# Exponentials of two scales in one operation, and the channels of a chunk taken in fours

## The chip, the cores and the metric

The kernel runs on one core of one Trainium2 chip. The time is device time in microseconds (us), the median of several executions. The engines are TensorE (PE; its weight loads are PEld in the profile), VectorE (DVE), ScalarE (ACT), GpSimd (POOL) and SyncE (SP), which issues transfers. Each engine has its own queue of instructions and works through it in order.

## The reference, cut to what matters

Two independent halves are computed and laid side by side in the output. Half A is attention over 8 positions with a dilation of 2, between two projections. Half B, which the change touches, is a long convolution whose kernel is made from 192 complex exponentials per channel:

```python
# A: x (2048, 640), 32 heads of 20;  idx = pos - 2*[0..7], masked where negative
logits = einsum("bhsd,bhswd->bhsw", q, k[idx]) * scale
a = (einsum("bhsw,bhswd->bhsd", softmax(logits), v[idx])) @ wo
# B: u (2048, 640); A_re, A_im, B_*, C_* (640, 192); log_dt, Dskip (640)
dt = exp(log_dt)
P = exp(dt * (A_re + 1j * A_im) * l)            # l = 0 .. 2047
K = einsum("dn,dnl,dn->dl", C, P, dt * B).real  # (640, 2048)
y = irfft(rfft(pad(u)) * rfft(pad(K)))[:2048]   # causal convolution per channel
b = y + u * Dskip
out = concatenate([a, b], -1)
```

## The kernel before

**Tiling.** The 640 channels of half B are worked in five chunks (`NCH = 5`) of 128. Channels lie in four groups g of 160; a chunk c takes 32 channels of each group, counted by u (4) and t (8), and a parameter tile holds channel (g, t) of quarter u on partition 32u + 8g + t. Before the change channel number = 160g + 40u + 5t + c, so that one partition's five chunks lie side by side in memory.

**Prologue** (`partB_prep` and its `fill`, lines 86 to 199). The parameters are loaded; log_dt gives dt (dtb, dtc), a diagonal DG = identity times dt, and TensorE's product of DG with `B_A_re` transposes and scales it into `alpha` (L149 to L155). `B_A_im` becomes phases, cut in three bf16 pieces (`hi`, `mid`, `lo`) that transfers move into the tile `LP` (L170). The products of B and C become coefficients `cn` (L189 to L193), transposed into `cT`. `fill(0, 1, ...)` does chunk 0 and `fill(1, NCH, ...)` the other four; both are traced before the chunk loop, and their instructions interleave.

**Tables of a chunk.** A power of the exponential is factored into tables, so that the 2048 powers need not be evaluated one by one: `exps_chunk` (L213) writes the real part R, one ScalarE exponential of 128x192 for each of 45 scales, and `trig_half` (L226) writes sines TA and TX of half a chunk from phases that TensorE computes (ps_ph). R and the sines need different tables of ScalarE's functions, so a table load stands before each.

**Kernel generation.** `small_half` (L265) multiplies tables into P, Q, F, G and X on VectorE, for half a chunk at a time. For each of the two quarters of a half, `y_form` (L299) makes three Y's, and `kgen_unit` (L309) contracts Y with X on TensorE (ps_k), and ScalarE copies the result to Ksb. The tag "Y" has four buffers, shared with Q; P has one buffer under the tag "P".

**Transforms.** `fwd` (L327) takes u or K through two steps of matmuls (ps_f), each followed by four ScalarE copies, A and Sg. `products` (L348) multiplies the spectra on VectorE, `inverse_a` (L364) goes half-way back into Z, stored to memory. `times_d` (L382) writes u times Dskip (UD) on VectorE, in ten pieces over chunks 0 to 3. After the loop the attention half runs on the same engines, with the last step of the inverse transform (`Inverse.part`, L642) in between; that step's matmuls (ps_ib) add UD.

**The order of the work.** The framework plans each engine's order ahead of time from dependences and estimated durations; `keep_in_program_order` holds an instruction at its place in the program, and `issue_after` holds a block's instructions behind a given one on the same engine. In the loop (L719 to L762) the exponentials of chunk c+1 are issued after the sines of the second half of chunk c, and the sines of chunk c+1's first half after those exponentials. In chunk 0 the matmuls of `unit(0, 1, 0)` are held behind those of the transform of u (L756). A tile takes over a buffer only when the readers of the tile before it have finished.

Of the kernel before, what the change touches and what calls it, by code (L numbers as in the profile page):

```python
# [10 lines left out]
A = mybir.AluOpType  # L11
# [5 lines left out]
NCH = 5  # L17
# [34 lines left out]
    return F1, F64  # L52


R_MULT = [float(a) for a in range(8)] + [8.0 * b for b in range(8)] + [64.0 * (16 + i) for i in range(16)] + [64.0 * (31 - i) for i in range(16, 32)]
L1_OF_ROW = [16 + i for i in range(16)] + [31 - i for i in range(16, 32)]


# [27 lines left out]
def partB_prep(tc, pools, prm):  # L86
# [9 lines left out]
    alpha = flat[:, 9824:11744].bitcast(f32).rearrange("p (c u w) -> p c u w", c=NCH, u=4)  # L96
    V.memset(flat[96:128, 0:7680].bitcast(f32), 1.0019378662109375)
    ldt = pa.tile([128, NCH], bf16, name="ldt")
    lsrc = prm["B_log_dt"].rearrange("(g u t c) -> u g t c", g=4, u=4, t=8)
    late = tc.keep_in_program_order  # L100
    one = pa.tile([128, 2], f32, name="one")
    nc.gpsimd.memset(one[:], 0.0)
# [2 lines left out]
    nat = {}  # L105
    F1n, F64n = table_consts_np()

    def load(nm):
        nat[nm] = (pa if nm == "B_A_im" else pb).tile([128, NCH, 192], bf16, name=nm, tag=nm)
        src = prm[nm].rearrange("(g u t c) n -> u g t (c n)", g=4, u=4, t=8)  # L110
        for u in range(4):
            queue = {"B_A_re": (nc.scalar, nc.sync)[u % 2], "B_A_im": nc.gpsimd, "B_B_im": nc.gpsimd, "B_C_im": nc.gpsimd}.get(nm, nc.sync)
            late(queue.dma_start(out=nat[nm][32 * u:32 * u + 32].rearrange("p c n -> p (c n)"), in_=src[u]))

    load("B_A_re")
    load("B_A_im")
    late(nc.sync.dma_start(out=CF1, in_=inline(nc, F1n, "c_F1")))
    late(nc.sync.dma_start(out=CF64, in_=inline(nc, F64n, "c_F64")))
    late(nc.scalar.activation(out=one[:], in_=one[:], func=ACT.Exp))
    for nm in ("B_B_re", "B_B_im", "B_C_re", "B_C_im"):  # L120
        load(nm)
# [13 lines left out]
    def fill(c0, c1, between):  # L135
# [60 lines left out]
            nc.scalar.copy(out=cT[:, c0:c1, 12 * u:12 * u + 12, 0:3:2], in_=ps.rearrange("p c w (q f) -> p c q w f", f=4))  # L196

        transposed(coefficients, cn, lambda sl, c: id32[sl, :])
    return dict(CF1=CF1, CF64=CF64, LP=LP, alpha=alpha, cT=cT), fill


def coefficients(engine, B, c):
# [7 lines left out]
        engine.tensor_copy(out=co[:, :, 3], in_=co[:, :, 0])  # L210


def exps_chunk(tc, pools, B, c):  # L213
    nc = tc.nc
    R = pools["tab"].tile([128, 48, NE_R, 4], bf16, name="R", tag=f"R{c % 2}")
    src = B["alpha"][:, c].rearrange("p u (q f) -> p (u q) f", f=4)
    nc.gpsimd.memset(R[:, :, 0:16:8, :], 1.0)
    nc.gpsimd.memset(R[:, :, 47, :], 1.0)
    for e, m in enumerate(R_MULT):
        if m == 0.0:  # L220
            continue
        nc.scalar.activation(out=R[:, :, e, :], in_=src, func=ACT.Exp, scale=m)  # L222
    return R


# [83 lines left out]
def kgen_unit(tc, pools, u, X, Ys, Ksb):  # L309

    nc = tc.nc
    MM = nc.tensor.matmul
    ps = pools["psum"].tile([128, 8, 64], f32, name="ps_k", tag="bank", bufs=2)
    for k in range(3):
        for t in range(8):
            for g in range(4):
                q, f = divmod(8 * g + t, 4)
                MM(ps[32 * g:32 * g + 32, t], lhsT=X[:, q, 2 - k, :, f], rhs=Ys[k][:, q, :, f], start=(t == 0 and k == 0), stop=False, tile_position=(0, 32 * g), skip_group_check=True)  # L318
        for t in range(8):
            for g in range(4):  # L320
# [61 lines left out]
def times_d(tc, pools, C, UDd, c, i):  # L382

    nc = tc.nc
    U = C["U"][:].rearrange("p l (ut c) -> p c l ut", c=NCH)[:, c]
    UD = pools["tabb"].tile([128, 32, 32], bf16, name="UD", tag="UD")
    tc.keep_in_program_order(nc.vector.tensor_tensor(out=UD[:], in0=U[:, 32 * i:32 * i + 32], in1=bc(C["Dsb"][:, c], 1, 32), op=A.mult))
    nc.sync.dma_start(out=UDd[c, :, 1024 * i:1024 * i + 1024], in_=UD[:].rearrange("p l j -> p (l j)"))


def fwd_u(tc, pools, C, Sd, c):

    U = C["U"][:].rearrange("p l (ut c) -> p c l ut", c=NCH)[:, c]
    Su, last = fwd(tc, pools, C, (lambda ut: U[:, :, ut]), 0, pools["fft"])
    tc.nc.sync.dma_start(out=Sd[c], in_=Su[:].rearrange("p a b c -> p (a b c)"))
    return last

# [221 lines left out]
class Inverse:  # L619
# [12 lines left out]
    def load(self, qr, c0=0, c1=NCH):  # L632
        nc = self.nc
        pool, tag = ((self.a2, "Z"), (self.att.ta, "LPC"), (self.att.a1, "prod"), (self.att.ta, "U"))[qr]
        if c0 == 0:
            self.t[qr] = pool.tile([96, 4, NCH, 16, 32], bf16, name="Z", tag=tag)
        for c in range(c0, c1):
            for ri in range(3):
                src = self.UDd[c, :, 512 * qr:512 * qr + 512] if ri == 2 else self.Zd[c, :, 2048 * ri + 512 * qr:2048 * ri + 512 * qr + 512]
                (nc.sync, nc.gpsimd)[(c + ri) % 2 if qr in (0, 3) else 0].dma_start(out=self.t[qr][32 * ri:32 * ri + 32, :, c].rearrange("p g l n -> p g (l n)"), in_=src.rearrange("(g p) n -> p g n" if ri == 2 else "(p g) n -> p g n", g=4))  # L640

    def part(self, l0, n):  # L642
        nc = self.nc
        qr, l = divmod(l0, 16)
        lo = l0 % 8
        if lo == 0:
            self.ysb = self.ysbs[:, l0 // 8 % 4]
        ysb = self.ysb
        ps = self.att.one("ps_ib")
        for i in range(n):  # L650
            for g in range(4):
                self.att.MM(ps[32 * g:32 * g + 32, 160 * i:160 * i + 160], lhsT=self.HB[:, l0 + i, :], rhs=self.t[qr][:, g, :, l + i, :], start=(i == 0), stop=True, skip_group_check=True, tile_position=(0, 32 * g))
        nc.scalar.copy(out=ysb[:, lo:lo + n].rearrange("p l (ut c) -> p l ut c", c=NCH), in_=ps[:, 0:160 * n].rearrange("p (l c ut) -> p l ut c", l=n, c=NCH))
# [8 lines left out]
def body(tc, ctx, pools, prm, B_u, B_Dskip, Sd, Zd, UDd, A_x, A_wqkv, A_wo, out_a, out_b):  # L662
# [14 lines left out]
    with tc.tile_pool(name="prep_b", bufs=1) as pb, tc.tile_pool(name="prep_c", bufs=1) as pc, tc.tile_pool(name="prep_a", bufs=1) as pa, tc.tile_pool(name="psum_p", bufs=2, space=bass.MemoryType.PSUM) as psp:  # L677
        pools.update(prep_a=pa, prep_b=pb, prep_c=pc)
        B, fill = partB_prep(tc, dict(pools, psum=psp), prm)
        fill(0, 1, lambda u: None)  # L680
        Dn = pa.tile([128, 160], bf16, name="Dn")
        dsrc = B_Dskip.rearrange("(g ch) -> g ch", g=4)
        late = tc.keep_in_program_order
        late(nc.sync.dma_start(out=BD[:].rearrange("p a b n -> p (a b n)"), in_=inline(nc, cn["BD"], "c_BD")))
        late(nc.sync.dma_start(out=EA[:].rearrange("p a n -> p (a n)"), in_=inline(nc, cn["EA"], "c_EA")))
        late(nc.sync.dma_start(out=T2[:].rearrange("p a n -> p (a n)"), in_=inline(nc, cn["T2"], "c_T2")))
        for g in range(4):
            late(nc.sync.dma_start(out=Dn[32 * g:32 * g + 32, :], in_=dsrc[g].partition_broadcast(32)))
# [5 lines left out]
        nc.gpsimd.tensor_copy(out=Dsb[:], in_=Dn[:].rearrange("p (ut c) -> p c ut", c=NCH))  # L694
# [24 lines left out]
    for c in range(NCH):  # L719
# [88 lines left out]
    def fill(some, n=1):  # L808
        for f in some[0:n]:
            f()  # L810
        del some[0:n]
# [97 lines left out]
```

## Time and profile before

| What | us |
|---|---|
| median of 3 runs (439.4 to 442.8) | 439.51 |
| the profiled execution | 438.98 |
| its span, first to last instruction | 437.2 |
| VectorE busy | 391.3 (89%) |
| TensorE busy | 358.4 (82%) |
| ScalarE busy | 314.0 (72%) |
| GpSimd busy | 44.5 (10%) |

A row of the groups gives the line, engine, operation, the tiles written and read with their shapes, how often it ran, the busy time and the mean length of one, and what ended the idle time before it. A row of the timeline gives start, length, engine, line, operation and count. Queues of transfers appear as SPq or as DMA rows. A tile's name appears without its buffer's number, and tiles that share a buffer may appear under the first one's name: `alpha` and the tables of constants are shown as LPC.

### The profile page before, as it was taken

The numbers are of one execution on the slowest core, as the hardware profiler recorded it, in microseconds if no ns is written. First come the engines' busy times: TensorE is split into PE (matmuls) and PEld (weight loads), VectorE is DVE, ScalarE is ACT, GpSimd is POOL, SyncE is SP. The second block draws the span as 40 slices with busy tenths as digits, with TensorE's granted clock in tenths as the row PEclk, the third lists the DMA queues.
The fourth block names the chain that finished last, engine by engine and source line by source line (L and its number), as shares of the span: only waits on it lengthen the run. The fifth ranks groups of instructions, "written<-read, shape, count | busy, mean of one in ns | idle before, by whom it ended". The sixth has DMA issues, their size and how long they took to land.

```text
span 437.2 us, 17687 instructions
## 1 busy us (share of the span) xinstructions
PE 358.4 (82%) x8041; PEld 241.1 (55%) x8041; DVE 391.3 (89%) x386; ACT 314.0 (72%) x570; POOL 44.5 (10%) x85
## 2 busy tenths in 40 slices
PE   1397659989886998879778799999899897399995
PEld 0145546866863677556665665545555674134443
DVE  7889999999997999999999989946978989999751
ACT  3974998889999899979997845342858344544663
POOL 7440000000000000000010000400001204102110
PEclk9996577999999898889999899999999999659999
DMA  5569102163233402324079933500210907957343
GB/s 143 186 141 200 18 3 109 39 227 94 99 123 123 97 28 98 144 103 99 27 258 241 236 75 135 178 0 3 67 32 1 265 17 201 228 141 225 96 107 114
DMA packets 45131, 51.62 MB, mean 118 GB/s; under 512 B 31376, under 2 KB 38992, under 8 KB 42368
## 3 DMA queue, kind: packets, MB, share of 16 engines
q1 hardware_dynamic: 41520, 41.41, 35.4%
q0 software_dynamic: 3392, 8.95, 7.0%
q8 instruction: 63, 1.03, 1.0%
q10 hardware_dynamic: 144, 0.12, 0.1%
q14 instruction: 12, 0.10, 0.1%
HBM read 28.03 MB, written 18.35 MB: 106 GB/s over the span
## 4 chain that ended last, share of the span: by engine, by line
PE 49%; ACT 29%; DVE 14%; issue 5%; DMA 1%; SPq 1%; DVEq 0%; ACTq 0%
ACT R L222 10%; ACT A L338 6%; PE ps_k L318 6%; PE ps_ph L247 6%; PE ps_k L323 6%; PE ps_op L420 6%; PE ps_k L470 4%; PE ps_q L488 4%; PE ps_ph L250 4%; ACT Sg L344 4%; PE ps_f L343 4%; PE ps_v L501 2%; DVE prod L521 2%; ACT Z L375 2%; PE ps_o L420 2%
## 5 line engine op out<-in xcount | busy, mean ns | idle before, releaser
L305 DVE TENSOR_TENSOR Y<-F,G 128x3072 bf16<-128x3072 bf16 x60 | 102.9, 1751 | 0.6 <-PE ps_k L323 0.6
L222 ACT ACTIVATE R<-LPC 128x192 bf16<-128x192 f32 x225 | 59.3, 358 | 0.1
L247 PE MATMUL ps_ph<-LPC 128*128 128x256 bf16 (+1 forms) x200 | 41.5, 311 | 17.3 <-DMA LPC<-lo 8.7
L318 PE MATMUL ps_k<-Y,X 128*32 128x64 bf16 x1920 | 47.2, 239 | 7.3 <-DVE Y L305 3.8
L323 PE MATMUL ps_k<-Y,X 64*32 64x64 bf16 x1920 | 43.8, 233 | 3.4 <-issue 3.3
L344 ACT CAST Sg<-ps_f 128x1024 bf16<-128x1024 f32 x40 | 37.6, 1027 | 7.3 <-PE ps_f L343 7.3
L318 PEld LDWEIGHTS <-X 128*32 128x32 bf16 x1920 | 32.1, 117 | 17.4 <-issue 9.0
L343 PE MATMUL ps_f<-A,T 128*128 128x128 bf16 x320 | 27.3, 259 | 14.9 <-ACT A L338 14.2
L338 ACT CAST A<-ps_f 128x1024 bf16<-128x1024 f32 x40 | 37.6, 1036 | 0.7 <-PE ps_f L337 0.6
L271 DVE TENSOR_TENSOR X<-R,TX 128x1536 bf16<-128x1536 bf16 x40 | 36.4, 951 | 0.0
L323 PEld LDWEIGHTS <-X 64*32 64x32 bf16 x1920 | 29.6, 113 | 12.1 <-issue 4.4
L255 ACT ACTIVATE TX<-ps_ph 128x864 bf16<-128x864 int16 (+1 forms) x40 | 31.9, 867 | 5.3 <-DVE X L271 2.5
L343 PEld LDWEIGHTS <-T 128*128 128x128 bf16 x320 | 25.6, 119 | 16.1 <-issue 14.9
L585 DVE TENSOR_TENSOR prod<-v,atp 128x2048 bf16<-128x2048 bf16 (+2 forms) x32 | 31.3, 1018 | 2.0 <-PE ps_o L420 1.8
L255 ACT ACTIVATE TA<-ps_ph 128x768 bf16<-128x768 int16 x40 | 30.6, 822 | 3.4 <-PE ps_ph L250 3.0
L250 PE MATMUL ps_ph<-LPC 128*64 128x128 bf16 (+1 forms) x400 | 29.6, 249 | 0.0
L247 PEld LDWEIGHTS <-LPC 128*128 128x128 bf16 x200 | 15.0, 102 | 25.9 <-issue 19.1
L420 PE MATMUL ps_op<-wo,o 128*128 128x320 bf16 x160 | 28.5, 315 | 0.8 <-ACT o L595 0.4
L358 DVE TENSOR_TENSOR P<-P,Sg 128x4096 bf16<-128x4096 bf16 x10 | 22.9, 2288 | 4.1 <-DMA P<-Sdram 3.2
L250 PEld LDWEIGHTS <-LPC 128*64 128x64 bf16 x400 | 15.2, 118 | 19.1 <-issue 18.9
L611 ACT CAST ob<-ps_op 128x320 bf16<-128x320 f32 x28 | 11.9, 431 | 19.0 <-PE ps_op L420 17.3
L337 PE MATMUL ps_f<-BD,U 128*64 128x128 bf16 x320 | 19.4, 285 | 6.1 <-ACT A L338 3.3
(129 smaller groups left out, 661.2 us busy)
## 6 DMA issues: line engine op xcount, KB each, us to landing
Sdram<-Sg SPq DMA_DIRECT2D x5, 1024.0 KB
P<-Sdram SPq DMA_DIRECT2D x5, 1024.0 KB
P<-Sdram SPq DMA_DIRECT2D x10, 512.0 KB
Zdram<-Z SPq DMA_DIRECT2D x5, 1024.0 KB
Z<-Zdram SPq DMA_DIRECT2D x30, 128.0 KB
U<-in_B_u_dram SPq DMA_DIRECT2D x4, 640.0 KB
UDdram<-UD SPq DMA_DIRECT2D x10, 256.0 KB
out_dram<-ysb SPq DMA_DIRECT2D x32, 80.0 KB
```

The costliest lines, as they stand in the source:

```text
L222: nc.scalar.activation(out=R[:, :, e, :], in_=src, func=ACT.Exp, scale=m)
L247: MM(o[:, :, 0:32], lhsT=L[:, 0:128], rhs=rhs, start=first, stop=last, skip_group_check=True)
L250: MM(o[64 * hh:64 * hh + 64, :, 32:48], lhsT=L[:, 128:192], rhs=rhs[:, :, 16 * hh:16 * hh + 16], start=False, stop=last, skip_group_check= ...
L255: last = nc.scalar.activation(out=dst[:, qs, e0:e0 + 2 * n, :].rearrange("p q (b e) f -> p b e q f", b=2), in_=words.rearrange("p b (e q f ...
L271: TT = lambda o, a, b, op: V.tensor_tensor(out=o, in0=a, in1=b, op=op)
L305: nc.vector.tensor_tensor(out=Y[:].rearrange("p q (b a) f -> p q b a f", a=8), in0=fa, in1=gb, op=A.mult)
L318: MM(ps[32 * g:32 * g + 32, t], lhsT=X[:, q, 2 - k, :, f], rhs=Ys[k][:, q, :, f], start=(t == 0 and k == 0), stop=False, tile_position=(0, ...
L323: MM(ps[32 * g:32 * g + 32, t], lhsT=X[hb, q, 2 - k, :, f], rhs=Ys[k][hb, q, :, f], start=False, stop=(k == 2), tile_position=(64 * (g // ...
L338: nc.scalar.copy(out=A1[:, :, 32 * b:32 * b + 32].rearrange("p k (j g) -> p k j g", g=4), in_=ps[:].rearrange("p j k g -> p k j g"))
L343: last = MM(ps[:, kk], lhsT=C["T2"][:, 8 * b + kk, :], rhs=A1[:, 8 * b + kk, :], start=(kk % 4 == 0), stop=True, skip_group_check=True)
L344: nc.scalar.copy(out=Sg[:, :, 8 * b:8 * b + 8, :], in_=ps[:].rearrange("p k (j g) -> p j k g", g=4))
L420: self.MM = lambda *a, **k: self.tc.keep_in_program_order(self.nc.tensor.matmul(*a, **k))
```

## The change

Four things are edited.

1. **Exponentials.** `R_MULT` goes. The 45 scales of a chunk are sorted into pairs (m, 2m) where both are wanted: 14 pairs and 17 single ones. A pair is one ScalarE operation of 128x384 that reads a new tile `twice`, which holds 2 x alpha and alpha, and writes two rows of R. `twice` is written by VectorE for chunk 0 and by GpSimd for chunks 1 to 4; for these it lies in the buffer of tag "P". The single ones are issued first and still read `alpha`.
2. **Channel order.** Channel number is now 160g + 20t + 4c + u. The u of four neighbours is therefore adjacent in the tile of u, of Dskip and of the output; the views of U, Dsb, Ksb, ps_ib and ysb are written accordingly, and log_dt and the parameters are read with other strides.
3. **Loads.** Each parameter's chunk 0 is one transfer over 128 partitions. Its chunks 1 to 4 follow in four transfers: those of `B_A_im` and `B_A_re` at once, those of B and C after the moves of chunk 0's pieces (`load_rest`).
4. **Queues.** `B_A_re` of chunk 0 goes to ScalarE's queue, its rest to SP's; the imaginary parts stay on GpSimd's.

```diff
-R_MULT = [float(a) for a in range(8)] + [8.0 * b for b in range(8)] + [64.0 * (16 + i) for i in range(16)] + [64.0 * (31 - i) for i in range(16, 32)]
...
-    lsrc = prm["B_log_dt"].rearrange("(g u t c) -> u g t c", g=4, u=4, t=8)
+    lsrc = prm["B_log_dt"].rearrange("(r c u) -> u r c", c=NCH, u=4)
...
+    def load(nm, queue, rest):
+        if not rest:
+            nat[nm] = (pa if nm == "B_A_im" else pb).tile([128, NCH, 192], bf16, name=nm, tag=nm)
+            late(queue.dma_start(out=nat[nm][:, 0], in_=prm[nm].rearrange("(r c u) n -> c u r n", c=NCH, u=4)[0]))
+        else:
+            src = prm[nm].rearrange("(r c u) n -> u r c n", c=NCH, u=4)
+            for u in range(4):
+                late(queue.dma_start(out=nat[nm][32 * u:32 * u + 32, 1:], in_=src[u, :, 1:]))
+    load("B_A_im", nc.gpsimd, False)
+    load("B_A_re", nc.scalar, False)
...
+    load("B_A_im", nc.gpsimd, True)
+    load("B_A_re", nc.sync, True)
+    def load_rest():
+        for nm, queue in (("B_B_re", nc.sync), ("B_C_re", nc.sync), ("B_B_im", nc.gpsimd), ("B_C_im", nc.gpsimd)):
+            load(nm, queue, True)
...
-def exps_chunk(tc, pools, B, c):
+def exps_chunk(tc, pools, B, c, engine, twice):
...
+    alpha = B["alpha"][:, c].rearrange("p u w -> p (u w)")
+    for b in range(2):
+        engine.tensor_scalar(out=twice[:, b], in0=alpha, scalar1=2.0 - b, scalar2=None, op0=A.mult)
...
-    for e, m in enumerate(R_MULT):
-        if m == 0.0:
-            continue
-        nc.scalar.activation(out=R[:, :, e, :], in_=src, func=ACT.Exp, scale=m)
+    one, two = [], []
+    for places in ({a: a for a in range(1, 8)}, {8 * a: 8 + a for a in range(1, 8)}, {64 * j: j if j > 15 else 47 - j for j in range(1, 32)}):
+        left = sorted(places)
+        while left:
+            m = left.pop(0)
+            e, step = places[m], 0
+            if 2 * m in left:
+                left.remove(2 * m)
+                step = places[2 * m] - e
+            (two if step else one).append((m, e, step))
+    for m, e, step in one + two:
+        src = twice[:].rearrange("p b (q f) -> p q b f", f=4)
+        if step == 0:
+            src, out = alpha.rearrange("p (q f) -> p q f", f=4), R[:, :, e, :]
+        elif step < 0:
+            out = R[:, :, e + step:e + 1:-step, :]
+        else:
+            src, out = src[:, :, ::-1, :], R[:, :, e:e + step + 1:step, :]
+        nc.scalar.activation(out=out, in_=src, func=ACT.Exp, scale=float(m))
...
-    nc.scalar.copy(out=Ksb[:, 8 * u:8 * u + 8, :], in_=ps[:])
+    nc.scalar.copy(out=Ksb.rearrange("p (t u) l -> p u t l", u=4)[:, u], in_=ps[:])
...
-    U = C["U"][:].rearrange("p l (ut c) -> p c l ut", c=NCH)[:, c]
+    U = C["U"][:].rearrange("p l (t c u) -> p c l t u", c=NCH, u=4)[:, c]
...
-        fill(0, 1, lambda u: None)
+        fill(0, 1, lambda u: B["load_rest"]() if u == 3 else None)
...
-        R[0] = exps_chunk(tc, pools, B, 0)
+        R[0] = exps_chunk(tc, pools, B, 0, nc.vector, pa.tile([128, 2, 192], f32, name="twice"))
...
+            twice = pools["tabb"].tile([128, 2, 192], f32, name="twice", tag="P")
             with tc.issue_after(trig[c, 1][2].ins):
                 coefficients(nc.scalar, B, c + 1)
-                R[c + 1] = exps_chunk(tc, pools, B, c + 1)
+                R[c + 1] = exps_chunk(tc, pools, B, c + 1, nc.gpsimd, twice)
```

More of the change, by code (lines that the diff above doesn't have):

```diff
@@ L106, in partB_prep @@
     F1n, F64n = table_consts_np()
[L108 to L116, printed above, removed]
+    def load(nm, queue, rest):
[8 more added lines that the diff above has]
+    load("B_A_re", nc.scalar, False)
+    late(nc.scalar.activation(out=one[:], in_=one[:], func=ACT.Exp))
     late(nc.sync.dma_start(out=CF1, in_=inline(nc, F1n, "c_F1")))
     late(nc.sync.dma_start(out=CF64, in_=inline(nc, F64n, "c_F64")))
-    late(nc.scalar.activation(out=one[:], in_=one[:], func=ACT.Exp))
-    for nm in ("B_B_re", "B_B_im", "B_C_re", "B_C_im"):
-        load(nm)
+    for nm, queue in (("B_B_re", nc.sync), ("B_B_im", nc.gpsimd), ("B_C_re", nc.sync), ("B_C_im", nc.gpsimd)):
+        load(nm, queue, False)
+    load("B_A_im", nc.gpsimd, True)
[3 more added lines that the diff above has]
+            load(nm, queue, True)
     dtb = pa.tile([128, NCH], bf16, name="dtb")
@@ L198, in fill @@
         transposed(coefficients, cn, lambda sl, c: id32[sl, :])
-    return dict(CF1=CF1, CF64=CF64, LP=LP, alpha=alpha, cT=cT), fill
+    return dict(CF1=CF1, CF64=CF64, LP=LP, alpha=alpha, cT=cT, load_rest=load_rest), fill
 def coefficients(engine, B, c):
@@ L210, in coefficients @@
         engine.tensor_copy(out=co[:, :, 3], in_=co[:, :, 0])
-def exps_chunk(tc, pools, B, c):
+def exps_chunk(tc, pools, B, c, engine, twice):
     nc = tc.nc
     R = pools["tab"].tile([128, 48, NE_R, 4], bf16, name="R", tag=f"R{c % 2}")
-    src = B["alpha"][:, c].rearrange("p u (q f) -> p (u q) f", f=4)
+    alpha = B["alpha"][:, c].rearrange("p u w -> p (u w)")
+    for b in range(2):
+        engine.tensor_scalar(out=twice[:, b], in0=alpha, scalar1=2.0 - b, scalar2=None, op0=A.mult)
     nc.gpsimd.memset(R[:, :, 0:16:8, :], 1.0)
     nc.gpsimd.memset(R[:, :, 47, :], 1.0)
-    for e, m in enumerate(R_MULT):
-        if m == 0.0:
-            continue
-        nc.scalar.activation(out=R[:, :, e, :], in_=src, func=ACT.Exp, scale=m)
+    one, two = [], []
[17 more added lines that the diff above has]
+        nc.scalar.activation(out=out, in_=src, func=ACT.Exp, scale=float(m))
     return R
@@ L384, in times_d @@
     nc = tc.nc
-    U = C["U"][:].rearrange("p l (ut c) -> p c l ut", c=NCH)[:, c]
+    U = C["U"][:].rearrange("p l (t c u) -> p c l t u", c=NCH, u=4)[:, c]
     UD = pools["tabb"].tile([128, 32, 32], bf16, name="UD", tag="UD")
-    tc.keep_in_program_order(nc.vector.tensor_tensor(out=UD[:], in0=U[:, 32 * i:32 * i + 32], in1=bc(C["Dsb"][:, c], 1, 32), op=A.mult))
+    tc.keep_in_program_order(nc.vector.tensor_tensor(out=UD[:].rearrange("p l (t u) -> p l t u", u=4), in0=U[:, 32 * i:32 * i + 32], in1=bc(C["Dsb"][:, c].rearrange("p (t u) -> p t u", u=4), 1, 32), op=A.mult))
     nc.sync.dma_start(out=UDd[c, :, 1024 * i:1024 * i + 1024], in_=UD[:].rearrange("p l j -> p (l j)"))
 def fwd_u(tc, pools, C, Sd, c):
-    U = C["U"][:].rearrange("p l (ut c) -> p c l ut", c=NCH)[:, c]
-    Su, last = fwd(tc, pools, C, (lambda ut: U[:, :, ut]), 0, pools["fft"])
+    U = C["U"][:].rearrange("p l (t c u) -> p c l t u", c=NCH, u=4)[:, c]
+    Su, last = fwd(tc, pools, C, (lambda tu: U[:, :, tu // 4, tu % 4]), 0, pools["fft"])
     tc.nc.sync.dma_start(out=Sd[c], in_=Su[:].rearrange("p a b c -> p (a b c)"))
@@ L651, in part @@
             for g in range(4):
-                self.att.MM(ps[32 * g:32 * g + 32, 160 * i:160 * i + 160], lhsT=self.HB[:, l0 + i, :], rhs=self.t[qr][:, g, :, l + i, :], start=(i == 0), stop=True, skip_group_check=True, tile_position=(0, 32 * g))
-        nc.scalar.copy(out=ysb[:, lo:lo + n].rearrange("p l (ut c) -> p l ut c", c=NCH), in_=ps[:, 0:160 * n].rearrange("p (l c ut) -> p l ut c", l=n, c=NCH))
+                self.att.MM(ps[32 * g:32 * g + 32, 160 * i:160 * i + 160].rearrange("p (t c u) -> p c t u", c=NCH, u=4), lhsT=self.HB[:, l0 + i, :], rhs=self.t[qr][:, g, :, l + i, :], start=(i == 0), stop=True, skip_group_check=True, tile_position=(0, 32 * g))
+        nc.scalar.copy(out=ysb[:, lo:lo + n].rearrange("p l ch -> p (l ch)"), in_=ps[:, 0:160 * n])
         if lo + n == 8:
@@ L693, in body @@
         fill(1, NCH, lambda g: late(nc.sync.dma_start(out=U[32 * g:32 * g + 32], in_=usrc[g])))
-        nc.gpsimd.tensor_copy(out=Dsb[:], in_=Dn[:].rearrange("p (ut c) -> p c ut", c=NCH))
+        nc.gpsimd.tensor_copy(out=Dsb[:].rearrange("p c (t u) -> p c t u", u=4), in_=Dn[:].rearrange("p (t c u) -> p c t u", c=NCH, u=4))
     psg = ctx.enter_context(tc.tile_pool(name="psum_g", bufs=2, space=bass.MemoryType.PSUM))
```

## The prediction

> **What bounds the kernel now.** I read the page's busy line, then VectorE's and ScalarE's rows in time order through the chunk loop, then GpSimd's rows, then the groups by shape.
>
> From the page, and from the table of waits:
>
> ```profile
> PE 358.4 (82%) x8041; PEld 241.1 (55%) x8041; DVE 391.3 (89%) x386; ACT 314.0 (72%) x570; POOL 44.5 (10%) x85
> ...
> DVE P L271 <- ACT TA L255: 3.0, 1, 3.0
> ```
>
> From 33.87 us (the first product P of chunk 0) to 283.5 us, the end of the last Y, VectorE starts nearly every instruction before the one ahead has ended; its gaps there sum to some 6 us, the longest the 3.0 above. VectorE sets the pace of the loop, with ScalarE just behind: P of chunk c+1 waits for tables TA that ScalarE writes after the exponentials. P starts at 33.87, 75.72, 133.35, 184.28 and 233.99 us in the five chunks.
>
> VectorE, then ScalarE, where chunk 1 is prepared (start, length, line):
>
> ```profile
> 56.52 1.75 DVE L271 TENSOR_TENSOR Q<-P,cT 128x3072 bf16<-128x3072 bf16 x1
> ...
> 71.15 1.32 DVE L387 TENSOR_TENSOR UD<-U,Dsb 128x1024 bf16<-128x1024 bf16 x1
> 72.39 3.42 DVE L305 TENSOR_TENSOR Y<-F,G 128x3072 bf16<-128x3072 bf16 x2
> 75.72 0.95 DVE L271 TENSOR_TENSOR P<-R,TA 128x1536 bf16<-128x1536 bf16 x1
> ...
> 57.25 4.16 ACT L222 ACTIVATE R<-LPC 128x192 bf16<-128x192 f32 x16
> 61.31 3.72 ACT L338 CAST A<-ps_f 128x1024 bf16<-128x1024 f32 x4
> 71.20 2.30 ACT L255 ACTIVATE TA<-ps_ph 128x768 bf16<-128x768 int16 x3
> ```
>
> Behind the 16 exponentials on ScalarE's queue stand the copies A of the transform of u; TensorE's next matmuls ps_k stand behind that transform; VectorE's fifth Y of six needs the buffer of the first Y (there are four), which those matmuls free. So exponentials that start late stop all three engines.
>
> GpSimd's rows that read SBUF, and VectorE's beside them:
>
> ```profile
> 25.44 0.95 DVE L191 TENSOR_TENSOR p<-p,p 128x768 f32<-128x768 f32 x1
> 26.42 1.18 DVE L193 TENSOR_SCALAR cn<-p,dtc 128x192 bf16<-128x192 f32 x4
> ...
> 25.15 1.80 POOL L209 TENSOR_SCALAR cT<-cT 128x192 bf16<-128x192 bf16 x1 [0.54 <-ACT cT L196]
> 26.92 0.34 POOL L210 COPY cT<-cT 128x192 bf16<-128x192 bf16 x1
> ...
> 65.48 0.42 POOL L217 MEMSET R<- 128x384 bf16 x1 [35.72 <-DVE X L271]
> ...
> 276.74 6.75 DVE L305 TENSOR_TENSOR Y<-F,G 128x3072 bf16<-128x3072 bf16 x4
> 279.80 3.98 POOL L481 COPY kT<-kT 128x280 bf16<-128x280 bf16 x1 [5.74 <-ACT kT L471]
> ```
>
> A copy of 192 elements takes 0.34 us. The copy of 280 at 279.80 took 3.98 us and ended at 283.78, 0.29 after VectorE's run of tensor_tensors ended at 283.49; two instruction ends inside the run did not let it in. The tensor_scalar at 25.15 likewise sat through the end of one tensor_tensor and ended 0.56 us after the last (26.39). The memset, which reads nothing, took 0.42 under the same load.
>
> **The change, part by part.**
>
> *Exponentials.* 45 per chunk become 17 singles and 14 pairs. Before, 45 take 11.49 us, 0.255 each in a row (0.358 alone). The softmax exponential of 2048 elements takes 1.91, so an element costs (1.91-0.358)/1856 = 0.84 ns and a pair 0.255+192x0.84 ns = 0.415. New: 17x0.255+14x0.415 = 10.1 us, 1.35 less per chunk. Bounds per pair: 0.255 (nothing for the second half) to 0.51 (no gain).
>
> *The doubled copies "twice".* A pair reads a tile of two scaled copies of alpha. In chunk 0 VectorE writes it (two tensor_scalars, 0.25 each by L177). For chunks 1 to 4 GpSimd does, reading SBUF, into the buffer of P, so after Q of the half before: in chunk 1 not before 58.3 us. Each operation alone: between 0.34 (L210) and 0.56 (the end of L209 after its release); I take 0.45, 0.9 for two. On GpSimd's queue nothing urgent is behind them; on ScalarE's everything above.
>
> I take the kT row as the rule: these reads wait until VectorE has nothing to run. Then, on the clock of before (chunk by chunk):
>
> - Chunk 1. VectorE runs on from Q to the fifth Y, which it reaches at 74.06, less 0.65 for UD (below): 73.4. It stops there, since ScalarE stands at the first pair. GpSimd finishes at 74.3, 14 pairs at 80.1, four copies A (3.72) at 83.8, where before they ended at 65.03: 18.8 later. The first Y's matmuls, done near 73.1 before, are done at 91.9; fifth Y to 93.6; TA's third copy (73.5) comes at 92.3. P starts at 93.6 instead of 75.72: **+17.9**.
> - Chunk 2. VectorE, 2.5 ahead by three UDs and the 0.57 us gap of 76.7, reaches a fifth Y (125.67) before TensorE has read the first (124.57, plus 0.9 of lag). GpSimd uses that gap, at about 123.1 to 124; ScalarE wants the pairs at about 123.5. Pairs 5.8, table load 1.28, three TA 2.4: P at 133.5: **+0.2**. Without the gap it would be about +4.
> - Chunk 3. Two pairs are queued ahead of the copies Sg, so TensorE stops in the transform, VectorE at its fifth Y (179.7 less two UDs, 178.4). GpSimd 0.9, two pairs 0.8, Sg 3.8, twelve pairs 5.0, load 1.28, TA 2.4: P at 192.6, not 184.28: **+8.3**.
> - Chunk 4, the same from 230.65 less two UDs, 229.3: P at 243.4, not 233.99: **+9.4**.
>
> *u in fours.* UD's inner run becomes 4 adjacent values instead of a stride of 5. L387 takes 1.344 us for 1024 elements; L518, 1024 adjacent ones, 0.689. I take 0.69: 0.65 less on VectorE, ten times, counted in the stops above; the other end is nothing. TensorE's weight loads of U keep their stride of 160. The strided PSUM writes of ps_ib and the now contiguous copy to ysb I cost at nothing: L250 writes runs of 16 in rows of 48 and takes 249 ns, and Ksb's contiguous copy of 512 takes 580 where ysb's of 480 takes 563.
>
> *Loads.* Chunk 0's slice of each parameter comes as one 48 KB transfer, the rest after chunk 0's moves to LP. B_A_re's last quarter, landed at 9.11, no longer holds the first exponential (9.79). But log_dt now comes in pieces of 2 bytes: 640 instead of 128. At 60 ns a packet (2476 us of engine time over 41520 packets of q1), 512 more on 16 engines are up to 1.9 us; I take 1.0 (0 to 1.9). Two identity copies and tx now precede DG on VectorE, 0.6. The first exponential starts at about 10.1. ScalarE's work to the end of TX of chunk 0: 4.3+5.8 exponentials, 0.3 waiting for twice, 1.1 cT copies, 1.28 load, 3.1 TA, 0.5 alpha copies, 3.2 TX: 29.7 (30.76 before). But the order now has TX's negation ahead of 5.7 us of coefficient work (four products and sums at 0.87, eight cn at 0.27) that filled the wait before. P of chunk 0: 29.7+0.6+5.8 = 36.1, not 33.87: **+2.2**. SP's and GpSimd's later rest loads (about 27 us for the last, by 20.6 issued plus B_C_im's 5.8) and U (needed at 56, some 10 us of slack) hide behind that. Bounds -1.5 (log_dt at no cost, negation no hindrance) to +5.
>
> **Sum:** 2.2+17.9+0.2+8.3+9.4 = 38.0 us on the profiled run of 438.98 (span 437.2): 477. That run is 0.5 below the median of 439.51; behind chunk 4 nothing changes. Within the case: prep -1.5 to +5, chunk 2 up to +4, chunks 3 and 4 by 2 us each as gaps fall, pairs and UD at their dear ends +6 each, GpSimd at 0.34 to 0.56 one us: about 464 to 486.
>
> **Rivals.**
>
> 1. *GpSimd gets in at the next instruction end.* Then twice is ready at 59.2, the pairs end at 65.0 (61.41 before, +3.6), P of chunk 1 at +2.7. After that ScalarE gains 1.35 and VectorE 1.3 to 2.6 a chunk: about -3.7 over chunks 2 to 4. With +2.2 of prep: **440**, not slower. For it: only one copy shows the long block. Against: three boundaries (25.44, 280.08, 281.75), none won. [...]
> 2. *It gets in at the negation of TX* (60.46), a tensor_scalar, where no row shows GpSimd losing. Twice at 61.4, pairs 67.2, P of chunk 1 +4.9, regained in part as above: **442**. A wait of a few us in each chunk gives 445 to 464.
> 3. *Not what it says:* a pair costs two singles and UD stays: 1.35x5 and 6.5 us back, **486** with the forecast's stops.
> 4. *Both gains reach the end and prep costs nothing:* UD 6.5 less what ScalarE cannot follow, less the late start of chunk 1: about **434**.
>
> **Chances.** Forecast 0.68; rival 3 inside its upper end; 445 to 464 0.08; rivals 1 and 2 0.18; rival 4 0.06. One per cent, 4.4 us, is about what measurement of this kernel tells from no change. Slower by over that 0.76, within it 0.16, faster 0.08. The range must reach the rivals' times: 440 to 486; the forecast's own is 464 to 486.
>
> **What the profile will show.** Right: two tensor_scalars on GpSimd in chunks 1, 3 and 4 many us long, ending when VectorE falls idle; ScalarE's wait ahead of the first pair released by GpSimd, about 15 us in chunk 1; VectorE idle at the fifth Y and before P. Wrong: those rows under 1 us, P of chunk 1 near 80. Pairs near 0.415, UD near 0.69, P of chunk 0 near 36 test the rest.

## The result, and the profile after

| | before | after |
|---|---|---|
| median of 6 runs each, us | 440.19 (438.2 to 442.8) | 482.21 (480.0 to 487.0) |
| ratio, with its 95% interval | | 1.096 (1.089 to 1.103) |
| profiled execution / its span, us | 438.98 / 437.2 | 480.73 / 479.0 |

The kernel is 9.6% slower. The forecast was 477.0 within 440 to 486, slower with a chance of 0.76. On the clock of the profiled executions it said +38.0 us; they lie 41.75 apart.

From the page of the changed kernel, its busy line and three groups:

```profile
PE 361.8 (76%) x8041; PEld 241.7 (50%) x8041; DVE 387.4 (81%) x388; ACT 308.7 (64%) x500; POOL 96.7 (20%) x96
...
L333 DVE TENSOR_TENSOR Y<-F,G 128x3072 bf16<-128x3072 bf16 x60 | 103.1, 1749 | 40.0 <-PE ps_k L351 40.0
L229 POOL TENSOR_SCALAR twice<-LPC 128x192 f32<-128x192 f32 x8 | 50.7, 6345 | 170.8 <-DVE Q L299 170.8
L250 ACT ACTIVATE R<-twice 128x384 bf16<-128x384 f32 x70 | 30.0, 523 | 41.7 <-POOL twice L229 39.8
```

VectorE and ScalarE are busy for less than before (391.3 and 314.0 us there); the share of VectorE falls from 89% to 81%. Its idle time ahead of Y was 0.6 us and is 40.0; the group of Y before was:

```profile
L305 DVE TENSOR_TENSOR Y<-F,G 128x3072 bf16<-128x3072 bf16 x60 | 102.9, 1751 | 0.6 <-PE ps_k L323 0.6
```

Eight operations of 192 elements on GpSimd are busy for 50.7 us, and ScalarE's pairs wait 39.8 for them.

From the table of waits of the changed kernel (total, times, longest):

```profile
DVE Y L333 <- PE ps_k L351: 40.0, 6, 18.3
...
ACT R L250 <- POOL twice L229: 39.8, 3, 17.9
...
PE ps_f L365 <- ACT A L366: 24.8, 6, 22.6
```

That is the circle of the prediction, each engine waiting for the next. It runs in chunks 1, 3 and 4; in chunk 2 ScalarE does not wait for GpSimd. Chunk 1, from the timeline: GpSimd, then VectorE, then ScalarE (start, length, and in brackets the idle time before):

```profile
61.06 16.29 POOL L229 TENSOR_SCALAR twice<-LPC 128x192 f32<-128x192 f32 x2 [29.10 <-DVE Q L299]
...
60.82 0.55 DVE L299 TENSOR_TENSOR G<-G 128x768 bf16<-128x768 bf16 x1
61.29 0.95 DVE L299 TENSOR_TENSOR F<-Q 128x1536 bf16<-128x1536 bf16 x1
...
74.39 1.75 DVE L333 TENSOR_TENSOR Y<-F,G 128x3072 bf16<-128x3072 bf16 x1
94.47 1.76 DVE L333 TENSOR_TENSOR Y<-F,G 128x3072 bf16<-128x3072 bf16 x1 [18.33 <-PE ps_k L351]
96.14 0.95 DVE L299 TENSOR_TENSOR P<-R,TA 128x1536 bf16<-128x1536 bf16 x1
...
58.86 0.59 ACT L352 CAST Ksb<-ps_k 128x512 bf16<-128x512 f32 x1 [2.38 <-PE ps_k L351]
77.38 5.89 ACT L250 ACTIVATE R<-twice 128x384 bf16<-128x384 f32 x14 [17.94 <-POOL twice L229]
83.18 3.71 ACT L366 CAST A<-ps_f 128x1024 bf16<-128x1024 f32 x4
```

GpSimd starts 0.16 us after Q ends and finishes at 77.35, 1.2 us after VectorE's run of instructions has ended at 76.14. The shortest of the eight takes 0.68 us, the longest 15.63: where a couple is held, its first instruction is the one that stands.

Where the 41.8 us of span arise, by the start of the first product P of each chunk:

| | chunk 0 | 1 | 2 | 3 | 4 | first attention product |
|---|---|---|---|---|---|---|
| before | 33.87 | 75.72 | 133.35 | 184.28 | 233.99 | 286.48 |
| after | 36.51 | 96.14 | 153.85 | 213.37 | 273.75 | 329.78 |
| added here | +2.6 | +17.8 | +0.1 | +8.6 | +10.7 | +3.5 |
| predicted | +2.2 | +17.9 | +0.2 | +8.3 | +9.4 | 0 |

From there to the end the changed kernel takes 1.5 us less (149.2 against 150.7).

### The profile page after: what moved, and what is told of

It reads as the page before. It is cut to its first block, busy times and chain, and to the rows that moved or that the text cites. A ratio compares the mean times of both kernels' runs of the same rounds, so it can differ in the third digit from the quotient of the medians.

```text
span 479.0 us, 17629 instructions
## 1 busy us (share of the span) xinstructions
PE 361.8 (76%) x8041; PEld 241.7 (50%) x8041; DVE 387.4 (81%) x388; ACT 308.7 (64%) x500; POOL 96.7 (20%) x96
## 5 line engine op out<-in xcount | busy, mean ns | idle before, releaser
L229 POOL TENSOR_SCALAR twice<-LPC 128x192 f32<-128x192 f32 x8 | 50.7, 6345 | 170.8 <-DVE Q L299 170.8
L250 ACT ACTIVATE R<-twice 128x384 bf16<-128x384 f32 x70 | 30.0, 523 | 41.7 <-POOL twice L229 39.8
L275 PE MATMUL ps_ph<-LPC 128*128 128x256 bf16 (+1 forms) x200 | 43.6, 325 | 10.4 <-ACT TX L283 7.3
L365 PEld LDWEIGHTS <-U 128*64 128x64 bf16 x320 | 18.7, 204 | 23.2 <-issue 22.6
L278 PEld LDWEIGHTS <-LPC 128*64 128x64 bf16 x400 | 15.6, 121 | 21.8 <-issue 21.7
```

What stands on the lines that cost most here:

```text
L229: engine.tensor_scalar(out=twice[:, b], in0=alpha, scalar1=2.0 - b, scalar2=None, op0=A.mult)
L275: MM(o[:, :, 0:32], lhsT=L[:, 0:128], rhs=rhs, start=first, stop=last, skip_group_check=True)
L278: MM(o[64 * hh:64 * hh + 64, :, 32:48], lhsT=L[:, 128:192], rhs=rhs[:, :, 16 * hh:16 * hh + 16], start=False, stop=last, skip_group_check= ...
L365: MM(ps[64 * ri:64 * ri + 64, j], lhsT=src_fn(8 * b + j), rhs=C["BD"][:, wh, ri, :], start=(j % 4 == 0), stop=True, skip_group_check=True, ...
```

## The experiments

The theory, from GpSimd's 16.26 and 16.29 us in the changed kernel: a GpSimd instruction that reads SBUF stands until VectorE has a pause, and ScalarE's pairs stand behind it. The rivals: the wait is for the buffer or the queue in which `twice` lies; or the pairs, the loads or the channel order cost the time. Ratios are to the kernel before on the same chip, with 95% intervals.

| run | median, us | ratio |
|---|---|---|
| memset_twice | 444.13 | 1.006 (1.002 to 1.010) |
| singles | 448.24 | 1.017 (1.012 to 1.022) |
| scalar_twice | 448.09 | 1.015 (1.009 to 1.021) |
| pairs_alone | 491.15 | 1.117 (1.109 to 1.126) |
| early_double | 439.76 | 1.000 (0.996 to 1.004) |
| early_alone | 466.86 | 1.061 (1.054 to 1.069) |
| order_alone | 444.97 | 1.013 (1.006 to 1.019) |
| old_loads | 442.68 | 1.004 (0.999 to 1.009) |
| gap_given | 447.80 | 1.013 (1.005 to 1.020) |
| scalar_early | 443.82 | 1.003 (0.999 to 1.008) |
| pairs_scalar | 440.38 | 0.997 (0.993 to 1.002) |
| ud_alone | 439.37 | 0.996 (0.993 to 0.999) |

### GpSimd writes without reading

```diff
-        engine.tensor_scalar(out=twice[:, b], in0=alpha, scalar1=2.0 - b, ...)
+        engine.memset(twice[:, b], 0.0)      # chunks 1 to 4
```

> The changed kernel, but in chunks 1 to 4 GpSimd fills the two halves of twice with zeros by memsets instead of scaling alpha: same engine, same buffer, same place in the queues, but nothing is read from SBUF. It leaves out the doubled alpha of chunks 1 to 4, so their pairs exponentiate zeros. Theory (GpSimd's reads of SBUF wait until VectorE has nothing to run): the two memsets take under 1 us and end near 62 us in chunk 1; no stop of VectorE at the fifth Y; first products P of chunks 1 to 4 some 1 us either side of 77, 132, 182 and 232; total 435 (432 to 440), below the kernel before, since 6.5 us of UD fall away against 2.6 of preparation. Rival A (the wait is for the buffer of P, or for GpSimd's queue): the stops stay and the time is near 482. Rival B (the pairs themselves, or the loads, cost the time): near 482 as well, with P late without a stop of GpSimd.

The timeline of this run, GpSimd and ScalarE in chunk 1:

```profile
60.51 0.46 POOL L232 MEMSET twice<- 128x192 f32 x2 [29.01 <-DVE Q L302]
...
60.99 5.90 ACT L253 ACTIVATE R<-twice 128x384 bf16<-128x384 f32 x14 [2.00 <-POOL twice L232]
```

Two operations in the same buffer, behind the same Q, on the same queue: 0.46 us instead of 16.29, and 444.1 instead of 482.2 (a ratio of 1.006 instead of 1.096). So some 38 us belong to the read, or to the operation that does it, since a memset is another operation too; `gap_given` below keeps both. The total was expected at 432 to 440; it is 4 above that, and the rest of this section follows that up too. A part of it stands in the second line: ScalarE has used up its 17 single exponentials and waits 2.00 us here, because `twice` may be written only after Q has let go of the buffer of P.

### The exponentials undone

```diff
-            if 2 * m in left:
+            if False:                        # 45 single ones, no twice
```

> The changed kernel with its exponentials undone: 45 single ones per chunk that read alpha, no twice; channel order, loads and queues as changed. Theory: no stop, the time is that of before plus some 2.6 us in the preparation, less what of the 6.5 us of UD reaches the end: 437 (434 to 441). Rival B (loads or channel order cost the time): well above 445. A difference of this run to the one with memsets is what the pairs save on ScalarE's path, at most 1.35 us a chunk.

No stop, so neither loads nor order are the 42 us. But 448.2 misses the expected 434 to 441: order, loads and queues together, with UD down to 0.68 us, do not gain; they cost some 6 to 7 us (a ratio of 1.017).

### ScalarE writes twice, in the same place

```diff
+            engine.activation(out=twice[:, b], in_=alpha, func=ACT.Copy, scale=2.0 - b)
```

> The changed kernel, but in chunks 1 to 4 ScalarE itself writes twice, two copies with a scale of 128x192, into the same buffer just ahead of the pairs. All of the change's computation is done. Theory: no engine waits for another; two copies of about 0.26 us each more on ScalarE; total 436 (433 to 440), so the change without GpSimd is level with the kernel before or a little faster. Rival A (the buffer of P is what is waited for): ScalarE waits for VectorE's Q ahead of the first copy in each chunk, some us, and the time is above 445. Rival B (pairs, loads or order cost the time): near 482.

The timeline of ScalarE in this run, chunk 1:

```profile
58.10 0.59 ACT L355 CAST Ksb<-ps_k 128x512 bf16<-128x512 f32 x1 [2.38 <-PE ps_k L354]
60.18 0.62 ACT L232 ACTIVATE twice<-LPC 128x192 f32<-128x192 f32 x2 [1.49 <-DVE Q L302]
60.83 5.90 ACT L253 ACTIVATE R<-twice 128x384 bf16<-128x384 f32 x14
```

The stops are gone (448.1); the expected 433 to 440 is missed by 8. The rival on the buffer has a small part: 1.49 us for Q, and 2.38 ahead of the Ksb copy at 58.10. Before, exponentials filled both waits.

### The pairs alone, on the kernel before

The edit: the new `exps_chunk` with its calls in the kernel before, nothing else.

> The kernel before with the new exponentials alone: pairs that read twice, written by VectorE for chunk 0 and by GpSimd for chunks 1 to 4 into the buffer of P; channel order, loads and queues as before. Theory: the stops are all there, VectorE stands at the fifth Y in the chunks in which GpSimd is held: 483 (470 to 492). Where GpSimd gets in at once, as it did in chunk 2 of the changed kernel, a chunk costs nothing, so each chunk is either about 0 to 2 us or 8 to 18. Rival B (loads or order cost the time): within 1 per cent of before, 436 to 443.

Here all four chunks stop (16.85 to 21.44 us on GpSimd), and the time is higher than with the whole change. GpSimd in chunks 1 and 2, from the timeline of this run:

```profile
59.88 16.87 POOL L220 TENSOR_SCALAR twice<-LPC 128x192 f32<-128x192 f32 x2 [27.16 <-issue]
...
131.45 21.44 POOL L220 TENSOR_SCALAR twice<-LPC 128x192 f32<-128x192 f32 x2 [54.14 <-DVE Q L290]
```

Chunk 1 to 2, by the starts of P, takes 66.2 us where it took 57.6 before and 57.7 in the changed kernel, in which GpSimd was let in at once (below).

### A pause made for GpSimd

```diff
+    # on VectorE, behind F = Q0 + Q1
+    nc.vector.tensor_copy(out=scrap[:], in_=twice[:, 1, 0:1])
```

> The changed kernel with a pause made for GpSimd: behind Q's first sum F on VectorE stands a copy of one element of twice, so VectorE must wait there for GpSimd's two tensor_scalars. GpSimd, its buffer and its read of SBUF are as in the changed kernel. Theory (GpSimd is let in only when VectorE stands still): the two take about 1 to 2.5 us in every chunk, VectorE stands 0.5 to 2 us at that copy and no more at the fifth Y than in the run with ScalarE's copies; P of chunk 1 near 81; total 449 (444 to 455), some 33 us under the changed kernel though VectorE got more to do and a wait. Rival (the reads are slow of themselves beside the other engines' traffic): twice still 16 us long, VectorE stands for it at the copy, total 480 or more.

GpSimd and VectorE in chunk 1, from the timeline of this run:

```profile
60.70 2.39 POOL L257 TENSOR_SCALAR twice<-LPC 128x192 f32<-128x192 f32 x2 [28.80 <-DVE Q L305]
...
60.94 0.94 DVE L305 TENSOR_TENSOR F<-Q 128x1536 bf16<-128x1536 bf16 x1
63.13 0.15 DVE L787 COPY scrap<-twice 128x1 f32<-128x1 f32 x1 [1.25 <-POOL twice L257]
```

VectorE is given one instruction more in a chunk and made to wait 1.25 us there (0.59 in chunk 2), and the kernel becomes 34 us faster than the changed one: 447.8. The reads take 1.85 to 2.39 us in the four chunks. This shows the cause from the other side: the same operation and the same read, let in by a pause. In chunk 2 its first read was in before the pause, as in the changed kernel (below).

### The same read, a chunk earlier

GpSimd writes only the doubled alpha of chunk c+1, over alpha of chunk c, which is dead by then.

```diff
+def double(engine, B, c):
+    engine.tensor_scalar(out=B["alpha"][:, c], in0=B["alpha"][:, c + 1], scalar1=2.0, ...)
...
+        twice = B["alpha"][:, c - 1:c + 1]
```

> The whole change, with one thing moved: for chunks 1 to 4 GpSimd writes only the doubled alpha of chunk c+1, and writes it over alpha of chunk c, which lies just ahead of it and is dead once chunk c's exponentials are done. A pair reads the two neighbours; nothing lies in the buffer of P, and GpSimd has about a chunk's time instead of none. Same engine, same read of SBUF, same computation. Theory (GpSimd is held while VectorE runs without a pause, and that costs only when ScalarE waits for it): a doubling still takes up to some 16 us where VectorE runs on, but nobody waits for it; the wait of ScalarE for Q in chunk 1, 1.5 to 3.9 us in the runs with memsets and with ScalarE's copies, goes too; P of chunk 1 at 77 to 78; total 443 (438 to 448). Rival (a GpSimd that reads slows VectorE or ScalarE whenever it runs): stops or stretched instructions elsewhere, above 455.

> The kernel before with pairs in this early form alone: doubled alpha written over the chunk before by GpSimd, channel order, loads and queues as before. Theory: no stop; chunk 0 starts 1.4 us later, as in the run with pairs alone (P at 35.32), and ScalarE has 1.35 us less work a chunk: 440 (436 to 444), within one per cent of before.

> The early form of the pairs with the channel order in fours, and the loads and queues of before. Against the early form with the change's loads it tells what the loads cost. If they cost the 2 us of the preparation: 441 (436 to 445). If 384-byte pieces over all chunks load no faster than the change's slices: the same time as that run.

GpSimd, then VectorE, in the run with the whole change (`early_double`):

```profile
63.08 41.90 POOL L260 TENSOR_SCALAR LPC<-LPC 128x192 f32<-128x192 f32 x1 [30.42 <-ACT R L254]
...
178.57 4.11 POOL L260 TENSOR_SCALAR LPC<-LPC 128x192 f32<-128x192 f32 x1 [7.80 <-ACT R L254]
...
103.75 0.68 DVE L424 TENSOR_TENSOR UD<-U,Dsb 128x1024 bf16<-128x1024 bf16 x1
104.57 2.29 DVE L395 TENSOR_TENSOR P<-P,Sg 128x4096 bf16<-128x4096 bf16 x1
...
182.04 1.10 DVE L308 TENSOR_TENSOR P<-R,TA 128x1536 bf16<-128x1536 bf16 x1
```

One instruction of 192 elements stands for 41.9 us and costs nothing, for nobody needs it yet: 439.8, level with before, 42 us under the changed kernel with the same kind of read on the same engine (one instruction a chunk instead of two). It ends 0.55 us after the UD of 103.75 has ended (104.43), and the next VectorE row starts 0.14 after that end, the first gap since 63.08: a pause that short seems to be enough.

The same code on the kernel before (`early_alone`), GpSimd and ScalarE:

```profile
62.22 40.99 POOL L251 TENSOR_SCALAR LPC<-LPC 128x192 f32<-128x192 f32 x1 [24.52 <-ACT R L245]
...
177.83 54.43 POOL L251 TENSOR_SCALAR LPC<-LPC 128x192 f32<-128x192 f32 x1 [5.04 <-ACT R L245]
...
232.30 4.24 ACT L245 ACTIVATE R<-LPC 128x384 bf16<-128x384 f32 x10 [21.88 <-POOL LPC L251]
```

440 was expected and 466.9 came: a slack of a whole chunk is not enough either. The doubling for chunk 4 stood 54.43 us, past 47 ends of VectorE instructions without a pause, and ScalarE waited 21.88 for it. In `early_double` the same doubling, released at 178.57, took 4.11 us: it ended 0.55 after the end of a UD at 182.13, beside a P that took 1.10 instead of 0.95. With the loads of before (`old_loads`, median 442.7) the profiled execution took 456.07; in it that doubling was held and ScalarE waited 17.60 for it:

```profile
179.83 49.75 POOL L250 TENSOR_SCALAR LPC<-LPC 128x192 f32<-128x192 f32 x1 [7.17 <-ACT R L244]
...
229.61 2.17 ACT L244 ACTIVATE R<-LPC 128x384 bf16<-128x384 f32 x5 [17.60 <-POOL LPC L250]
```

Whether the early form on GpSimd meets a stop thus differs from one kernel to the next with nothing changed in the read itself, and could not be foretold here. What the loads cost cannot be read from these runs: by medians `old_loads` lies 3 us above `early_double`, and `order_alone` 3 below `singles`.

### The same place, ScalarE as the writer

```diff
-                double(nc.gpsimd, B, c + 1)
+                double(nc.scalar, B, c + 1)  # activation Copy, scale 2.0
```

> The kernel before with pairs alone, the doubled alpha written by ScalarE as in the run above; channel order, loads and queues as before. It is early_alone with the writer's engine changed and nothing else in chunks 1 to 4. Theory: the stop of 22 us in chunk 4 goes: 440 (436 to 444), against 466.9. It also tells what the pairs are worth where nothing waits: up to 1.35 - 0.3 = 1.05 us of ScalarE a chunk, most of which VectorE hides.

> The whole change without GpSimd: ScalarE writes the doubled alpha of chunk c+1 over alpha of chunk c after chunk c's last exponential (one copy of 128x192), and both halves of chunk 0's twice. Theory: nothing waits; P of chunk 0 at about 35 (the changed kernel's ScalarE waited 1.92 us for VectorE's twice in chunk 0, and VectorE wrote two tensor_scalars); total 438.5 (435 to 442), and no run near 455, as one of the runs with GpSimd's early doubling and the old loads was. Whether it is below the kernel before by more than one per cent: I give it 1 in 4, since the 6.5 us that UD saves are taken back where TensorE's granted clock is lower.

`pairs_scalar` differs from `early_alone` only in who writes the doubled copies (in chunk 0 too): 440.4 against 466.9. With nothing to wait for, the pairs are worth about 1 us, which the interval does not tell from nothing: 0.997 (0.993 to 1.002). The whole change in this form is at 443.8, no faster than before; why it lies 4 us above `early_double`, where GpSimd does the doubling and VectorE chunk 0's `twice`, is not settled. No version tried is faster than the kernel before by 1%.

### Channel order alone, and UD alone

The first is the kernel before with the new numbering of channels, the second the kernel before with only this:

```diff
-    U = C["U"][:].rearrange("p l (ut c) -> p c l ut", c=NCH)[:, c]
+    U = C["U"][:, :, 32 * c:32 * c + 32]
```

> The kernel before with the channel order alone: fours in u, single exponentials, every parameter in four transfers over all chunks on the queues of before (its pieces are 384 bytes now instead of 1920, since a partition's chunks no longer lie side by side). If the loads of the change cost what the run with single exponentials lost (P of chunk 0 2.4 us late, 448.2 against 442.4): P of chunk 0 near 34.5 and a total at or below before, 440 (436 to 444). If the channel order costs it (TensorE, with VectorE's pace no longer the limit, at a lower granted clock: 0.84 and 0.85 in chunks 2 and 4 there, 0.92 and 0.97 before): 445 to 449.

> The kernel before with one thing done: UD reads 32 adjacent channels of u instead of 32 at a stride of 5, so each of its ten tensor_tensors should take 0.69 us instead of 1.34. It leaves out the right choice of channels (chunk c multiplies channels 32c to 32c+31 by its Dskip); nothing else differs. My prediction counted 0.65 us ten times on VectorE as time off the loop. If so: P of chunk 4 at 228 to 229 instead of 233.99, and a total 5 to 6.5 us below before, 435 to 436. Rival: VectorE's saved time is handed to waits for ScalarE's tables and for TensorE, whose granted clock is lower where VectorE runs ahead (in the whole change with early doubling P of chunk 4 came 4.5 us earlier counted from P of chunk 0, and the first half of chunk 4 then took 31.0 instead of 28.0): P of chunk 4 at 230 to 233, total 440 (437 to 443), within one per cent of before.

UD takes 0.68 to 0.69 us instead of 1.34 in both, 6.6 us less on VectorE. Alone it gives 0.996 (0.993 to 0.999), some 2 us: by its total, the rival of that expectation. The place differs from both: in the profiled execution, which at 444.32 lies above the median, P of chunk 4 starts at 234.92, no earlier than before. With the new order 445.0 comes out, not 440; there P of chunk 0 starts at 36.41, 2.5 late, after a wait of 2.31 for TensorE's transposes (ps_tr). Ahead of it only the loads' pieces have changed, 384 bytes instead of 1920 for the parameters and 2 for log_dt, so they are the likely cause of these 2.5 us; no run changes them alone.

The rest may go at TensorE. Windows of 4 us at the start of chunk 4 (after the length: busy time of PE, PEld, DVE, ACT, POOL with counts, then the granted clock, the share of the transfers, GB/s). The kernel before:

```profile
230.00:234.00 4.00, 3.11 (x92) 1.87 (x82) 4.00 (x4) 3.99 (x6) 0.00 (x0) 1.00 1.18 297
234.00:238.00 4.00, 4.00 (x138) 2.60 (x140) 4.00 (x6) 3.52 (x5) 0.00 (x0) 1.00 1.15 172
```

The run `early_double`, at the same place, and from its timeline TensorE's row just ahead of it:

```profile
230.00:234.00 4.00, 4.00 (x113) 2.25 (x113) 3.36 (x4) 2.94 (x5) 0.00 (x0) 0.62 1.23 216
...
229.94 0.59 PE L360 MATMUL ps_k<-Y,X 64*32 64x64 bf16 x26 [1.86 <-issue]
```

The changed kernel, around the stop of chunk 4 and behind it:

```profile
254.00:258.00 4.00, 0.00 (x0) 0.00 (x0) 4.00 (x4) 0.00 (x0) 4.00 (x1) 0.54 0.00 0
258.00:262.00 4.00, 0.00 (x0) 0.00 (x0) 1.34 (x1) 1.42 (x3) 4.00 (x4) 0.50 0.00 0
262.00:266.00 4.00, 3.53 (x42) 2.18 (x42) 0.00 (x0) 4.00 (x7) 0.32 (x1) 0.50 0.95 305
...
278.00:282.00 4.00, 4.00 (x54) 1.66 (x52) 3.60 (x4) 2.66 (x4) 0.00 (x0) 0.50 1.12 151
```

Before, TensorE had small pieces of work nearly all the time (3.11 and 4.00 of 4 us), at a granted clock of 1.00. In `early_double` VectorE is ahead, TensorE has pauses (1.86 us ahead of 229.94) and the clock is 0.62 in that window. P of chunk 4 starts at 232.25 there, 1.7 us earlier than before though chunk 0 started 2.8 later; then the first half of the chunk takes 31.0 us instead of 28.05, and the gain is gone. That the lower clock is what takes UD's gain was not tested by itself; the two go together in these profiles.

## Why the prediction was right, point by point

**The stop.** Right in its mechanism, its place and its size in chunk 1. On the clock of before, which is 2.64 us behind, VectorE's run ended at 73.5 (predicted 73.4), GpSimd at 74.7 (74.3), and P of chunk 1 started at 93.5 (93.6). The 3.75 us by which the whole sum is short lie mainly in chunk 4 (1.3), behind it (2.0) and in the preparation (0.4).

**GpSimd waits for VectorE to fall idle, not for the next instruction end.** Right in chunks 1, 3 and 4. One row of before, the copy to kT, had carried this. The runs show it with holds of 15.6 to 54.4 us for one instruction, past 14 to 47 ends of VectorE instructions, the negations of TX among them, so rivals 1 and 2 (440 and 442) fall as the rule; in chunk 2 the read went in as rival 1 says. The memset (0.46 us for two, where the two reads took 16.29) and the made pause (1.85 to 2.39 us for the same two reads) point to the read, or the operation that does it, beside a VectorE without a pause.

**Chunk 2.** The number was right (+0.1 against +0.2) and the reason wrong, so the number was luck. I had GpSimd use a gap before a fifth Y. That gap did not come: VectorE ran on from 127.16 to 150.11. GpSimd was released by Q at 130.65 and got in at once, with no pause of VectorE in the profile. GpSimd's rows of chunks 2 to 4, and VectorE's beside the first, from the timeline of the changed kernel:

```profile
130.83 1.85 POOL L229 TENSOR_SCALAR twice<-LPC 128x192 f32<-128x192 f32 x2 [52.92 <-DVE Q L299]
183.91 16.26 POOL L229 TENSOR_SCALAR twice<-LPC 128x192 f32<-128x192 f32 x2 [45.20 <-DVE Q L299]
244.29 16.26 POOL L229 TENSOR_SCALAR twice<-LPC 128x192 f32<-128x192 f32 x2 [43.56 <-DVE Q L299]
...
130.57 0.55 DVE L299 TENSOR_TENSOR G<-G 128x768 bf16<-128x768 bf16 x1
131.03 1.10 DVE L299 TENSOR_TENSOR F<-Q 128x1536 bf16<-128x1536 bf16 x1
132.06 0.69 DVE L299 TENSOR_TENSOR G<-G 128x768 bf16<-128x768 bf16 x1
```

The instructions and their distances are those of the other chunks; only F took 1.10 instead of 0.95 and the second G 0.69 instead of 0.55. The two reads ended at 131.67 and 132.69, each 0.55 us after the end of a VectorE instruction (the first G at 131.12, F at 132.13): they went in at instruction ends. ScalarE came to the pairs at 144.31 and found `twice` ready; a held read would have kept it until after 150. In `pairs_alone` the read was released 0.18 us after Q's end, as here, was held, and the chunk cost 8.6 us (66.2 against 57.6).

**Chunks 3 and 4.** +8.6 and +10.7 against +8.3 and +9.4: right, the second 1.3 short.

**Behind chunk 4 "nothing changes".** This step failed: +3.5 us between P of chunk 4 and the attention half, then -1.5 to the end. TensorE, from the timeline of the changed kernel, at the start of chunk 4:

```profile
271.65 0.29 PE L351 MATMUL ps_k<-Y,X 64*32 64x64 bf16 x6
276.37 0.24 PE L351 MATMUL ps_k<-Y,X 64*32 64x64 bf16 x3 [4.43 <-issue]
276.54 0.61 PE L275 MATMUL ps_ph<-LPC 128*128 128x256 bf16 x2
```

The same two ps_ph products before:

```profile
233.75 0.39 PE L247 MATMUL ps_ph<-LPC 128*128 128x256 bf16 x2
```

TensorE stood 4.43 us for nothing that the profile shows, so the cause of this pause stays open; then the two products took 0.61 us instead of 0.39, at a granted clock of 0.50 (276 to 278). ScalarE's fourth TA waited 3.90 for them and VectorE's G 3.69 for that. In `early_double` the window 230 to 234, with a pause of 1.86 us just ahead of it, shows 0.62. What sets the granted clock was not tested.

**The preparation.** +2.6 against +2.2, from terms that cancel: log_dt gave dt at 5.99, 0.2 later than before and not 1.0, and ScalarE waited 1.92 for chunk 0's `twice`, not 0.3, since VectorE reached it late. With that copy on ScalarE (`pairs_scalar` against `pairs_alone`) P of chunk 0 starts 1.1 earlier, at 34.23. TX was done at 30.3 (29.7), and its negation and the coefficient work behind it took 6.2 us (6.4).

**Sizes.** Fourteen pairs in a row take 5.89 us, 0.42 each (0.415); UD 0.68 (0.69). From VectorE's end the two tensor_scalars take 1.21 us (76.14 to 77.35) where I had 0.9; let in beside a running VectorE, 1.85. Two sums of the prediction do not come out as written: rival 3's 6.75 and 6.5 us on 477 give 490, not 486, and the terms named for the range, all at their dear ends, add some 19 us and give 496. The time lies inside either.

**Rival 4** (434, all gains reach the end): nothing tried without stops came below 439. The term that it and my sum share, UD's 0.65 us ten times taken off the loop, is worth some 2 us alone. In the forecast it did little harm, since there it only moved the stops forward.

## What to carry to other kernels

A small helper on an idle engine was not free here: a GpSimd tensor_scalar of 192 elements that reads SBUF took 0.69 us where VectorE stood (129.59 in `early_double`) and 15.6 to 54.4 us in the holds beside a VectorE without pauses. As an estimate from those holds, count such a read as lasting until VectorE's next pause, and ask who waits for it. Look for a GpSimd row in the profile that ended only when VectorE stopped; one carried this forecast, though it missed chunk 2, where the read got in. If such a read must stay, give it a consumer that is a VectorE instruction (`gap_given`, 447.8 instead of 482.2 us), or better give the work to an engine that was not held here, ScalarE (`pairs_scalar`, 440.4 where `early_alone` took 466.9), and do it early in a buffer that nobody else needs (`scalar_early`, 443.8 where `scalar_twice` took 448.1).

## What the runs showed of the hardware that I had not expected

- A single GpSimd instruction of 192 elements stood for 54.43 us, 49.75, 41.90 and 40.99 us beside a running VectorE; one went in at a pause of 0.14 us between two VectorE rows, and in `old_loads` one at a pause of 0.01 (79.99 to 80.00).
- Sometimes it gets in without a pause: at 130.83 in the changed kernel, 116.71 in `gap_given`, 178.57 (after 3.4 us) in `early_double`, and beside the first products of chunk 0 at 35.85 in `early_alone` and 37.88 in `old_loads`. The VectorE instruction that started meanwhile then took some 0.15 us longer. In these places as in the long holds, the first read to get in ended 0.54 to 0.56 us after the end of a VectorE instruction. What decides at which end it gets in was not found.
- Ten VectorE instructions, 6.6 us shorter together, on the engine that was 89% busy, gave 2 us.
